# GpSimd copies for part of the V strips, and a last output tile in two column halves, in an attention and MLP kernel on one core

## The chip, the core and the metric

The kernel runs on one core of one Trainium2 chip. The metric is the device time of one execution in microseconds; lower is better. The core has five engines with a queue of instructions each: TensorE (PE, with its weight loads as PEld), VectorE (DVE), ScalarE (ACT), GpSimd (POOL) and SyncE (SP). Transfers are issued from the queues of POOL and SP and run on 16 DMA engines. Each engine takes its queue in order.

## The reference

For 8 batches with 8 heads of 64 there are 32 global and 512 local positions. A global query sees all 544 keys. A local query sees the 32 global keys and the local keys at most 32 positions away. The result, 4352 rows of 512, goes through a two-layer MLP (512 to 2048 to 512).

```python
k_all = np.concatenate([k_g, k_l], axis=2)
v_all = np.concatenate([v_g, v_l], axis=2)
out_g = np.matmul(sm(scale * np.matmul(q_g, k_all.transpose(0, 1, 3, 2))), v_all)
mask = np.abs(pos[:, None] - pos[None, :]) <= 32
s_ll = np.where(mask, scale * np.matmul(q_l, k_l.transpose(0, 1, 3, 2)), -1e9)
s_lg = scale * np.matmul(q_l, k_g.transpose(0, 1, 3, 2))
out_l = np.matmul(sm(np.concatenate([s_lg, s_ll], axis=-1)), v_all)
x = np.concatenate([out_g, out_l], axis=2)   # then batch and position as rows, heads as columns
h = x @ w_in
out = (h * np.clip(h + 3.0, 0.0, 6.0) / 6.0) @ w_out
```

## The kernel before, in words

The kernel first writes down all operations of all batches with their dependencies, an estimated duration, and a key that says when each is due (`add`). A planner (`Plan.lay`) then plays them through with one clock per engine and a model of the two transfer queues and sorts them by start. The program is issued in that order, so each engine's order is fixed when the kernel is built: a longer duration in an `add` moves other operations, on other engines too. Buffers come from rings (`acq`, `rel`): an operation that takes a buffer waits for the last reader of the one before.

Work goes by batch. Per batch:

- POOL issues the loads (`load`, L411): queries and keys of four tiles of 128 positions into `nat`, V into `ve` (the global rows `v_g` in partitions 0 to 31 of block 0, then five blocks of local rows; the fifth is a rest of 32 rows), and for every second batch the global queries and keys into `natg`. The weights `win` and `wout` come in four quarters each, through the same queue, in the first 65 us. A semaphore lane stands behind each load, and there are eight: a load waits until the eighth load before it has landed.
- Queries and keys are turned so that the head's dimension lies in the partitions: for batches 0 to 3 by PE transposes (L592, L612), for batches 4 to 7 by transfers (L582, `TURN_QK = 4`).
- A query tile of 128 is seen as four units of 32. Each unit needs the 32 global rows and 96 local rows of V in the 128 partitions of one "strip". The strips of a batch, 16 in all, stand in `st` (two buffers of 128 partitions x 16 x 512 fp16). `strips_moved` (L526) fills them for batches 1 to 7 with seven transfers from `ve` issued by SP (L536): one that repeats the global rows 16 times in partitions 0 to 31 (512 packets of 1 KB), and for each unit c the local rows (packets of 4 KB), in two pieces where the rows come from two blocks. For unit 1 the rows lie in partitions 32 to 127 of `ve` and go to the same partitions of `st`. Batch 0 has its own way (`strips_kept`, and a part of `strips_moved`): copies by DVE and ACT, and transfers.
- `local_step` per tile: scores on PE (L662, L669), mask and row minimum on DVE (L681), exponentials on ACT (L692), scaling on DVE (L706, `tensor_tensor` with both inputs in SBUF), transposes of the weights (L713 on PE up to batch 4, then L724 by transfers, `TURN_E = 5`), the product with the strips (L743) and its copy to `xt` on ACT or DVE (L296, L298).
- `global_steps`: the same for the 32 global queries, with scaling at L821, transposes at L835 and the product with `ve` at L848. When it and the strips are done, the batch's `ve` buffer is free for the batch after next.
- `moe_local`: the first layer (L870), ReLU on ACT (L877), the gate on DVE (L881), and the second layer (`second`, L892), 16 matmuls of 512 columns per tile of 128 positions, in four groups of four; the result is copied to `ot` (L296, L298) and stored by SP (L907).

After batch 7 `moe_global` does the global rows of all batches. In PE's order its matmuls stand between those of the last local tiles; the last tile of all is the fourth local tile of batch 7.

Of the kernel before, what the change touches and what calls it, by code (L numbers as in the profile page):

```python
# [79 lines left out]
class Plan:  # L80
# [128 lines left out]
def kernel(  # L209
# [24 lines left out]
    NU = P // UQ  # L234
# [3 lines left out]
    HD = H * D  # L238
# [15 lines left out]
    NS, NX, VE = 2, 3, 2  # L254
# [3 lines left out]
    psM = many(3, [P, 512], FP32, "m", pp)  # L258
# [6 lines left out]
    ve = many(VE, [P, NV, HD], FP16, "ve")  # L265
    st = many(2, [P, NJ * NU, HD], FP16, "st")
# [10 lines left out]
    ot = many(3, [P, dm], FP32, "ot")  # L277
    gs = many(2, [P, NDFF, 512], FP16, "gs")
# [4 lines left out]
    w_out_t = sb.tile([P, NDFF, dm], FP16, tag="wout", name="wout")  # L283
# [6 lines left out]
    add = plan.add  # L290
# [3 lines left out]
    def copy(op, out, in_):  # L294
        if op.eng == "ACT":
            nc.scalar.copy(out=out, in_=in_)  # L296
        else:
            nc.vector.tensor_copy(out=out, in_=in_)  # L298

    BOTH = ("ACT", "DVE")  # L300
# [225 lines left out]
    def strips_moved(b, js, key):  # L526
        r = b % 2
        n = len(js)
        j0, j1 = js[0], js[-1] + 1
        v4 = st[r].rearrange("p (u j) c -> p u j c", u=NU)  # L530
        before = [av_last[b - 2, j] for j in range(NJ)] if b >= 2 else []
        o = []

        def move(dst, src, packets, ns, deps):
            def emit(op):
                nc.sync.dma_start(out=dst, in_=src)  # L536
            o.append(add("SP", 600, emit, deps + before, key=key + 0.001 * len(o), dma=(packets, ns)))
            return o[-1]
        if n == NJ:
            move(st[r][0:G, :, :], ve[b % VE][0:G, 0:1, :].to_broadcast([G, NJ * NU, HD]), G * NJ * NU, SHORT, vload[b, 0][:1])  # L540
        elif n == NJ - KEEP or KEEP == 0 and j0 == 0:
            for j in range(j0, NJ) if KEEP else ():
                glob.append(move(v4[0:G, :, j, :], ve[b % VE][0:G, 0:1, :].to_broadcast([G, NU, HD]), G * NU, SHORT, vload[b, 0][:1]))
            if KEEP == 0:
                glob.append(move(st[r][0:G, :, :], ve[b % VE][0:G, 0:1, :].to_broadcast([G, NJ * NU, HD]), G * NJ * NU, SHORT, vload[b, 0][:1]))
        if b == 0:
            o += [x for x in glob if x not in o]
        ns = LONG if n == NJ else SHORT
        each = 1 if n == NJ else n
        for c in range(NU):  # L550
            lo = c * UQ
            a = min(P - lo, KL)
            deps = [x for j in range(j0, j1) for x in vload[b, j]]
            move(v4[G:G + a, c, j0:j1, :], ve[b % VE][lo:lo + a, j0:j1, :], a * each, ns, deps)
            if a < KL:
                deps = [x for j in range(j0 + 1, j1 + 1) for x in vload[b, j]]
                move(v4[G + a:P, c, j0:j1, :], ve[b % VE][0:KL - a, j0 + 1:j1 + 1, :], (KL - a) * each, ns, deps)
        return o
# [17 lines left out]
    TURN_M, TURN_QK, TURN_E, TURN_G, TURN = 1, 4, 5, 5, (64, 190.0, True)  # L576

    def turn_qk(b, j, ld, key, which=(0, 1)):
        r = b % 2
        if b >= TURN_QK:  # L580
            def move(op):
                nc.sync.dma_start_transpose(out=qk[r][:, :, :, UQ + j * P:UQ + (j + 1) * P].rearrange(  # L582
                    "d i p s -> d (i p) s"), in_=nat[ld[0].slot].rearrange("s i c -> s (i c)"))
            return add("SP", 1250, move, [*ld, prep["clear"], *old_qk(b, j)], key=key, rel=ld[:1], dma=TURN)
        w0, n = which[0], len(which)

        def pe(op):
            ps = psM[op.slot].bitcast(FP16) if b < TURN_M else psT[op.slot]
            for i in which:
                for p in range(NP):  # L590
                    c0 = ((i - w0) * NP + p) * P
                    nc.tensor.matmul(out=ps[:, c0:c0 + P], lhsT=nat[ld[0].slot][:, i, p * P:(p + 1) * P],  # L592
                                     rhs=ident, is_transpose=True)
        t = add("PE", 225 * n, pe, [*ld, prep["ident"]], key=key, acq="M" if b < TURN_M else "T", rel=ld[:1])

        def ev(op):
            ps = psM[t.slot].bitcast(FP16) if b < TURN_M else psT[t.slot]
            copy(op, qk[r][:, w0:w0 + n, :, UQ + j * P:UQ + (j + 1) * P],
                 ps[:, 0:n * NP * P].rearrange("d (i p s) -> d i p s", i=n, p=NP))
        deps = [t, prep["clear"]] + old_qk(b, j)  # L600
        return add(BOTH, (450 * n, 300 * n), ev, deps, key=key - 2, rel=[t])
# [33 lines left out]
    def local_step(b, j, key):  # L635
        r = b % 2
# [74 lines left out]
        def tr(op):  # L711
            for h in range(H):
                nc.tensor.matmul(out=psT[op.slot][:, h * P:(h + 1) * P], lhsT=pn[pn_op.slot][:, h, :],  # L713
                                 rhs=ident, is_transpose=True)
        if b < TURN_E:
            t = add("PE", 450, tr, scs, key=key - 0.2, acq="T", rel=[pn_op])
            et_op = add("DVE", 0, lambda op: None, [t], key=key - 0.3, acq="et")

            def ev(op):
                copy(op, et[et_op.slot].rearrange("k h q -> k (h q)"), psT[t.slot])  # L720
            e_ = add(BOTH, (900, 600), ev, [et_op], key=key - 2, rel=[t])
        else:
            def move(op):
                nc.sync.dma_start_transpose(out=et[op.slot], in_=pn[pn_op.slot].rearrange("q h k -> q (h k)"))  # L724
            e_ = et_op = add("SP", 1250, move, scs, key=key - 2, acq="et", rel=[pn_op], dma=TURN)
# [22 lines left out]
        else:  # L748
            vs = []
            for a in range(2):  # L750
                vs.append(add("PE", 235, lambda op, a=a: av(op, a), [e_, *strip[b, j], *vs], key=key - 0.4,
                              acq=f"A{a}", rel=[et_op]))
# [131 lines left out]
                                           op0=ALU.min, op1=ALU.mult)  # L884
        return add("DVE", 600, st_, [a], key=key - 1, rel=[f, to])

    def second(t0, gdone, set_, dests, keys):
        f = None
        for q in range(4):
            def pe(op, q=q):  # L890
                for c in range(q * 4, q * 4 + 4):
                    nc.tensor.matmul(out=psM[(f or op).slot], lhsT=gs[set_.slot][:, c, t0:t0 + P],  # L892
                                     rhs=w_out_t[:, c, :], start=(c == 0), stop=(c == NDFF - 1))
            deps = gdone[q * 4:q * 4 + 4] + [wo[q * 4]]
            if q == 0:
                f = s = add("PE", 865, pe, deps, key=keys[q], acq="M")
            else:
                s = add("PE", 865, pe, deps + [s], key=keys[q], rel=[set_] if q == 3 else [])
        oo = add("DVE", 0, lambda op: None, [s], key=keys[3] - 1, acq="ot")

        def ev(op):
            copy(op, ot[oo.slot], psM[f.slot])
        c = add(BOTH, (480, 605), ev, [oo], key=keys[3] - 1, rel=[f])

        for n, (dst, lo, hi) in enumerate(dests):
            def sto(op, dst=dst, lo=lo, hi=hi):
                nc.sync.dma_start(out=dst, in_=ot[oo.slot][lo:hi, :])  # L907
            add("SP", 600, sto, [c], key=keys[3] + 0.001 * n, rel=[oo], dma=(hi - lo, STORE))

    def moe_local(b, at, span):  # L910
        set_ = add("ACT", 0, lambda op: None, xdone[b, 0], key=at - 1, acq="gs")
        n = PART.get(b, 512)
        k, per, parts = 512 // n, n // P, Sl // n
        left = [0]

        def key():
            left[0] += 1
            return at + span * left[0] / 32
        done = [[None] * NDFF for _ in range(parts)]
        for part in range(parts):  # L920
            xdeps = [d for j in range(part * per, (part + 1) * per) for d in xdone[b, j]]
            for c in range(0, NDFF, k):
                o = first(c, n, part * n, lambda: xt[xt_op[b].slot], xdeps, [xt_op[b]], set_, key())
                done[part][c:c + k] = [o] * k
        for j in range(NJ):
            row = b * S + G + j * P
            second(j * P, done[j // per], set_, [(out[row:row + P, :], 0, P)], [key() for _ in range(4)])

    def moe_global(at, span):
        deps = [xgd[b] for b in range(B)]  # L930
# [122 lines left out]
```

## Time and profile before

| | us |
|---|---|
| median of 3 runs (332.3 to 334.16) | 332.98 |
| the profiled execution | 335.23 |
| its span, first to last instruction | 333.5 |
| PE busy | 317.4 (95%) |
| DVE busy | 265.2 (80%) |
| ACT busy | 253.9 (76%) |
| POOL busy, nearly all of it issuing loads | 106.1 (32%) |

The transfers moved 52.25 MB in 158,594 packets. The granted TensorE clock was 0.999 of full.

How to read the profile: "busy" is the time in which at least one instruction of the engine ran. A group is named by source line, engine, operation and tile (buffer numbers left out), with its count, mean duration, and the idle time of the engine ahead of it with what ended it. Each transfer has an issue (a short instruction on POOL or SP) and a landing. The chain that ended last goes back from the last instruction to what released it, and so on. The busy time of a matmul is modelled: matmuls overlap, and 16 matmuls of 512 columns, each shown with 0.38 us, follow each other at 0.216 us.

A row of the windows view names a stretch (from:to, length), then for PE, PEld, DVE, ACT and POOL the busy us and, in brackets, the number of instructions, then PE's granted clock, the load of the DMA engines and GB/s.

### The profile page before, as it was taken

The page shows a single profiled execution, that of the slowest core. Times are in us where ns is not written, and L with a number is a line of the kernel's source. Part 1 is how long each engine was busy: PE and PEld are TensorE (multiplying, and loading weights), DVE is VectorE, ACT ScalarE, POOL GpSimd, SP SyncE. Part 2 cuts the span into 40 slices and gives each one's busy share as a digit, 9 for nine tenths or more (in the row PEclk, how much of TensorE's full clock was granted, in tenths as well). Part 3 has the DMA queues.
Part 4 walks back from the last instruction along what each step waited for, and adds up shares of the span by engine and source line. Part 5 has one row for each costly group of instructions (what it writes and reads, how often), then busy time and mean ns, then how long its engine had stood idle before and what let it go on. Part 6 is the DMA issues. An engine that isn't in the chain of part 4 may idle for free.

```text
span 333.5 us, 10205 instructions
## 1 busy us (share of the span) xinstructions
PE 317.4 (95%) x3808; PEld 183.0 (55%) x3808; DVE 265.2 (80%) x997; ACT 253.9 (76%) x850; POOL 106.1 (32%) x139
## 2 busy tenths in 40 slices
PE   8989969799699999999999999999999999999995
PEld 6778855365356554555555555454455544546642
DVE  4899799789988799898998799689988896375400
ACT  4889798679789589977995689699988994474402
POOL 8724943198166733830760050005000000000000
PEclk9999999999999999999999999999999999999999
DMA  9999999999999999999999999999984215300022
GB/s 150 193 245 168 131 177 254 168 190 194 206 152 188 231 155 156 191 225 231 162 173 218 224 160 209 196 198 175 194 145 120 63 35 112 88 0 2 31 64 95
DMA packets 158594, 52.25 MB, mean 157 GB/s; under 512 B 142928, under 2 KB 151120, under 8 KB 158544
## 3 DMA queue, kind: packets, MB, share of 16 engines
q0 software_dynamic: 106560, 17.05, 71.9%
q1 hardware_dynamic: 51984, 34.55, 48.0%
q8 instruction: 30, 0.49, 0.6%
q14 instruction: 20, 0.16, 0.2%
HBM read 35.26 MB, written 8.91 MB: 132 GB/s over the span
## 4 chain that ended last, share of the span: by engine, by line
PE 60%; DMA 19%; POOL 7%; ACT 6%; DVE 5%; issue 2%; SPq 0%; ACTq 0%
PE m L892 28%; PE m L870 23%; DMA wout<-in_moe_w_out_dram 7%; DMA win<-in_moe_w_in_dram 5%; DMA nat<-in_k_l_dram 4%; POOL nat L411 3%; PE a L743 3%; POOL ve L411 3%; ACT sm L692 2%; DMA nat<-in_q_l_dram 2%; DVE gs L881 2%; PE s L669 2%; ACT t L877 1%; PE t L713 1%; PE s L662 1%
## 5 line engine op out<-in xcount | busy, mean ns | idle before, releaser
L892 PE MATMUL m<-wout,gs 128*128 128x512 f16 x544 | 129.6, 379 | 1.3 <-DMA wout<-in_moe_w_out_dram 1.3
L870 PE MATMUL m<-xt,win 128*128 128x512 f16 (+1 forms) x576 | 122.0, 355 | 1.7 <-DVE gs L881 1.0
L692 ACT ACTIVATE sm<-sm,stat 128x128 f32<-128x128 f32 x256 | 100.6, 397 | 11.4 <-DVE stat L681 10.8
L881 DVE SCALAR_TENSOR_TENSOR gs<-t,m 128x512 f16<-128x512 f32 x136 | 91.7, 683 | 19.6 <-ACT t L877 18.3
L877 ACT ACTIVATE t<-m 128x512 f32<-128x512 f32 x136 | 80.4, 597 | 22.1 <-PE m L870 21.3
L870 PEld LDWEIGHTS <-win 128*128 128x128 f16 x640 | 59.3, 98 | 52.2 <-issue 3.3
L892 PEld LDWEIGHTS <-gs 128*128 128x128 f16 x544 | 49.6, 98 | 52.7 <-issue 2.8
L681 DVE CUSTOM_DVE_ANT_0 sm<-s,mask 128x128 f32<-128x128 f32 x256 | 61.8, 283 | 2.5 <-PE s L669 1.1
L692 ACT ACTIVATION_READ_ACCUMULATOR sm<-sm,stat 128x1 f32 x256 | 49.6, 194 | 0.0
L706 DVE TENSOR_TENSOR pn<-sm,stat 128x512 f16<-128x512 f32 x64 | 44.0, 688 | 0.6
L411 POOL DMA_DIRECT2D ve<-in_v_l_dram x40 | 32.2, 822 | 15.0 <-PE m L870 4.3
L296 ACT CAST xt<-a 64x256 f16<-64x256 f32 (+1 forms) x83 | 31.0, 374 | 7.3 <-PE a L743 6.3
L411 POOL DMA_DIRECT2D nat<-in_q_l_dram x30 | 27.0, 899 | 23.1 <-DMA qk<-nat 10.2
L411 POOL DMA_DIRECT2D nat<-in_k_l_dram x30 | 27.4, 914 | 15.7 <-DMA nat<-in_k_l_dram 6.5
L743 PEld LDWEIGHTS <-st 128*128 128x128 f16 x448 | 19.7, 98 | 10.6 <-DVE et L298 0.3
L296 ACT COPY ot<-m 128x512 f32<-128x512 f32 x23 | 13.5, 588 | 13.8 <-PE m L892 10.5
L743 PE MATMUL a<-et,st 128*128 128x64 f16 x448 | 22.1, 193 | 0.2 <-ACT xt L296 0.2
L411 POOL DMA_DIRECT2D ve<-in_v_g_dram x8 | 4.8, 597 | 54.3 <-PE a L848 53.6
L681 DVE DVE_READ_ACCUMULATOR2_ANT stat<- 128x1 f32 x256 | 21.1, 83 | 0.0
L298 DVE CAST xt<-a 64x256 f16<-64x256 f32 (+1 forms) x33 | 14.1, 428 | 4.3 <-PE a L743 4.0
L702 DVE RECIPROCAL stat<-stat 128x4 f32<-128x4 f32 x64 | 11.1, 173 | 5.8 <-ACT sm L692 5.2
L807 ACT ACTIVATE sg<-a,stat 128x32 f32<-128x32 f32 x16 | 4.6, 287 | 14.3 <-DVE stat L798 14.3
(88 smaller groups left out, 279.6 us busy)
## 6 DMA issues: line engine op xcount, KB each, us to landing
out_dram<-ot SPq DMA_DIRECT2D x32, 256.0 KB, 3.7
st<-ve SPq DMA_DIRECT2D x14, 384.0 KB, 7.9
nat<-in_k_l_dram POOLq DMA_DIRECT2D x30, 128.0 KB, 8.1
nat<-in_q_l_dram POOLq DMA_DIRECT2D x30, 128.0 KB, 9.5
st<-ve SPq DMA_DIRECT2D x7, 512.0 KB, 7.7
st<-ve SPq DMA_DIRECT2D x14, 256.0 KB, 8.0
ve<-in_v_l_dram POOLq DMA_DIRECT2D x24, 128.0 KB, 6.0
st<-ve SPq DMA_DIRECT2D x18, 128.0 KB, 8.0
```

What stands on the lines that cost most here:

```text
L296: nc.scalar.copy(out=out, in_=in_)
L298: nc.vector.tensor_copy(out=out, in_=in_)
L411: nc.gpsimd.dma_start(out=dst(op), in_=src)
L681: nc.vector.tensor_tensor_reduce(out=sm[sm_op.slot][:, h, :], in0=psS[s.slot][:, e, p * P:(p + 1) * P], in1=m, scale=-scale, scalar=3.0e38 ...
L692: nc.scalar.activation(out=sm[sm_op.slot][:, h, :], in_=sm[sm_op.slot][:, h, :], func=EXP, scale=-1.0, bias=stat[stat_op.slot][:, 0, h:h + 1],
L702: nc.vector.reciprocal(out=stat[stat_op.slot][:, 2, h0:h1], in_=stat[stat_op.slot][:, 1, h0:h1])
L706: (nc.gpsimd if op.eng == "POOL" else nc.vector).tensor_tensor(out=pn[pn_op.slot][:, h0:h1, :], in0=sm[sm_op.slot][:, h0:h1, :], in1=stat[ ...
L743: nc.tensor.matmul(out=psA[a][:, c0:c0 + 64], lhsT=st[r][:, u * NJ + j, p * P:(p + 1) * P], rhs=et[et_op.slot][:, 2 * p:2 * p + 2, u * UQ: ...
L870: nc.tensor.matmul(out=psM[op.slot][:, i * n:(i + 1) * n], lhsT=w_in_t[:, m, (c + i) * P:(c + i + 1) * P], rhs=x()[:, m, t0:t0 + n], start ...
L877: nc.scalar.activation(out=t1[to.slot], in_=psM[f.slot], func=RELU, bias=0.5, scale=1.0 / 6.0)
L881: nc.vector.scalar_tensor_tensor(out=gs[set_.slot][:, c:c + k, t0:t0 + n], in0=t1[to.slot].rearrange("f (k t) -> f k t", k=k), scalar=1.0, ...
L892: nc.tensor.matmul(out=psM[(f or op).slot], lhsT=gs[set_.slot][:, c, t0:t0 + P], rhs=w_out_t[:, c, :], start=(c == 0), stop=(c == NDFF - 1))
```

## The change

In `strips_moved`, for batches 1 to 7, the transfer of the global rows becomes eight GpSimd copies, each to two of the 16 strips, and the transfer of unit 1's rows becomes four GpSimd copies (partitions 32 to 63 and 64 to 127, two tiles each). The planner takes them at 900 and 850 ns. Like the transfers they wait for the V loads and for the last reader of the strip buffer; they stand in POOL's queue, between the loads. The other five strip transfers stay on SP.

`second` can take a tile in several column parts. The last local tile of batch 7 is done in two halves of 256 columns: 16 matmuls, a copy and a store for each half, where 16 matmuls of 512 columns, one copy and one store were.

The tests at `TURN_QK` and `TURN_E` allow for fractions of a batch; both constants keep their values, 4 and 5.

```diff
@@ strips_moved
         if n == NJ:
-            move(st[r][0:G, :, :], ve[b % VE][0:G, 0:1, :].to_broadcast([G, NJ * NU, HD]), G * NJ * NU, SHORT, vload[b, 0][:1])
+            for i in range(0, NJ * NU, 2):
+                o.append(add("POOL", 900, lambda op, i=i: nc.gpsimd.tensor_copy(out=st[r][0:G, i:i + 2, :], in_=ve[b % VE][0:G, 0:1, :].to_broadcast([G, 2, HD])),
+                             vload[b, 0][:1] + before, key=key + 0.001 * len(o)))
...
             deps = [x for j in range(j0, j1) for x in vload[b, j]]
+            if c == 1 and n == NJ:
+                for x0, x1 in ((UQ, 2 * UQ), (2 * UQ, P)):
+                    for i in range(0, NJ, NJ // 2):
+                        o.append(add("POOL", 850, lambda op, x0=x0, x1=x1, i=i: nc.gpsimd.tensor_copy(
+                            out=v4[x0:x1, 1, i:i + NJ // 2, :], in_=ve[b % VE][x0:x1, i:i + NJ // 2, :]),
+                            deps + before, key=key + 0.001 * len(o)))
+                continue
             move(v4[G:G + a, c, j0:j1, :], ve[b % VE][lo:lo + a, j0:j1, :], a * each, ns, deps)
@@ turn_qk
-        if b >= TURN_QK:
+        if b + j / NJ >= TURN_QK:
@@ local_step
-        if b < TURN_E:
+        if b + j / NJ < TURN_E:
@@ second
-    def second(t0, gdone, set_, dests, keys):
+    def second(t0, gdone, set_, dests, keys, cuts=1):
+        w, oo, s, f = dm // cuts, None, None, None
+        for n in range(cuts):
+            cols = slice(n * w, (n + 1) * w)
...
+                        nc.tensor.matmul(out=psM[(f or op).slot][:, 0:w], lhsT=gs[set_.slot][:, c, t0:t0 + P],
+                                         rhs=w_out_t[:, c, cols], start=(c == 0), stop=(c == NDFF - 1))
...
+                copy(op, ot[oo.slot][:, cols], psM[f.slot][:, 0:w])
...
+                    nc.sync.dma_start(out=dst[:, cols], in_=ot[oo.slot][lo:hi, cols])
@@ moe_local
-            second(j * P, done[j // per], set_, [(out[row:row + P, :], 0, P)], [key() for _ in range(4)])
+            second(j * P, done[j // per], set_, [(out[row:row + P, :], 0, P)], [key() for _ in range(4)],
+                   2 if b == B - 1 and j == NJ - 1 else 1)
```

More of the change, by code (lines that the diff above doesn't have):

```diff
@@ L885, in first, with pe, ev, sto @@
         return add("DVE", 600, st_, [a], key=key - 1, rel=[f, to])
-    def second(t0, gdone, set_, dests, keys):
[L888 to L908, printed above, removed]
+    def second(t0, gdone, set_, dests, keys, cuts=1):
+        w, oo, s, f = dm // cuts, None, None, None
+        for n in range(cuts):
+            cols = slice(n * w, (n + 1) * w)
+            for q in range(4):
+                def pe(op, q=q, cols=cols, f=f if q else None):
+                    for c in range(q * 4, q * 4 + 4):
+                        nc.tensor.matmul(out=psM[(f or op).slot][:, 0:w], lhsT=gs[set_.slot][:, c, t0:t0 + P],
+                                         rhs=w_out_t[:, c, cols], start=(c == 0), stop=(c == NDFF - 1))
+                deps = gdone[q * 4:q * 4 + 4] + [wo[q * 4], s]
+                s = add("PE", 865 // cuts, pe, deps, key=keys[q] + 0.01 * n, acq=None if q else "M",
+                        rel=[set_] if q == 3 and n == cuts - 1 else [])
+                f = f if q else s
+            oo = oo or add("DVE", 0, lambda op: None, [s], key=keys[3] - 1, acq="ot")
+            def ev(op, cols=cols, f=f):
+                copy(op, ot[oo.slot][:, cols], psM[f.slot][:, 0:w])
+            c = add(BOTH, (480, 605) if cuts == 1 else (300, 340), ev, [oo, s], key=keys[3] - 1, rel=[f])
+            for i, (dst, lo, hi) in enumerate(dests):
+                def sto(op, dst=dst, lo=lo, hi=hi, cols=cols):
+                    nc.sync.dma_start(out=dst[:, cols], in_=ot[oo.slot][lo:hi, cols])
+                add("SP", 600, sto, [c], key=keys[3] + 0.001 * (n + i), rel=[oo], dma=(hi - lo, STORE))
```

## The prediction

> **What bounds the kernel now.** I read the page first, then the windows view (busy time by stretch of 20 us), then the waits, the timeline of TensorE (PE) and the chain that ended last.
>
> The windows, with busy us of PE, PEld, VectorE (DVE), ScalarE (ACT) and GpSimd (POOL) in each stretch:
>
> ```profile
> 40.00:60.00 20.00, 16.48 (x290) 11.43 (x288) 19.31 (x90) 17.86 (x69) 8.36 (x12) 1.00 1.27 209
> 60.00:80.00 20.00, 18.06 (x260) 10.82 (x259) 16.34 (x53) 15.35 (x53) 14.24 (x18) 1.00 1.79 177
> 80.00:100.00 20.00, 17.48 (x210) 9.86 (x209) 17.70 (x68) 16.91 (x57) 9.26 (x12) 1.00 1.76 183
> ...
> 120.00:140.00 20.00, 19.23 (x222) 10.31 (x219) 19.75 (x74) 18.67 (x63) 10.36 (x14) 1.00 1.89 164
> ...
> 160.00:180.00 20.00, 20.00 (x229) 10.81 (x228) 19.17 (x76) 18.49 (x65) 10.13 (x13) 1.00 1.92 175
> ```
>
> PE lacks 8.0 us between 40 and 100 us, and from 100 to 320 us it is nearly full (158.86 of 160 us between 100 and 260): there fewer transfers can buy nothing. So the gain, if any, lies before 100 us and behind the last matmul. The PE timeline says which idle time before 100 us is a transfer's:
>
> ```profile
> 44.73 0.44 PE L835 MATMUL t<-ident,pg 128*128 128x128 f16 x5 [1.49 <-ACT eg L296]
> 49.23 0.40 PE L713 MATMUL t<-ident,pn 128*128 128x128 f16 x4 [0.81 <-DVE pn L706]
> 50.49 0.35 PE L662 MATMUL s<-kgz,qk 128*128 128x32 f16 x8 [0.86 <-DVE stat L681]
> ...
> 64.39 2.75 PE L892 MATMUL m<-wout,gs 128*128 128x512 f16 x12 [1.32 <-DMA wout<-in_moe_w_out_dram]
> ...
> 91.25 0.40 PE L592 MATMUL t<-ident,nat 128*128 128x128 f16 x4 [2.34 <-DMA nat<-in_k_l_dram]
> ```
>
> Two waits are for loads: 1.32 us for the last quarter of w_out and 2.34 us for a key tile of batch 3. The three ahead of them are for ACT and DVE, which are full there. The chain shows how long both loads were under way (start, length):
>
> ```profile
> 42.27 22.07 DMA wout<-in_moe_w_out_dram
> ...
> 77.05 14.16 DMA nat<-in_k_l_dram
> ```
>
> A load that meets little traffic lands 3.3 us after its issue (the minimum over L411), so these two mostly stood in a queue: the DMA engines are 9 tenths busy there.
>
> **The change, part by part.** The times go with the profiled execution: 335.23 us, span 333.5 us, so 1.7 us lie around the span. It is 2.25 us above the median of 332.98; I put the difference that I work out on the median.
>
> *Removed.* In each of batches 1 to 7, SyncE (SP) no longer issues the 512 KB transfer of global rows and one 384 KB strip: 14 issues of some 0.6 us on a queue that is not late, and 896 of 2048 KB of strips per batch.
>
> *Added.* 12 copies on POOL per batch, of 1024 fp16 elements in each of 32 or 64 partitions. No copy on POOL is in the trace. The nearest rows:
>
> ```profile
> L374 POOL TENSOR_SCALAR_AFFINE_SELECT ident<-ident 128x128 f32<-128x128 f32 x1 | 0.3, 289 | 0.9 <-DVE ident L370 0.9
> L326 POOL TENSOR_SCALAR_AFFINE_SELECT mask<-mask 32x96 f32<-32x96 f32 x1 | 0.3, 258 | 0.0
> ...
> L298 DVE COPY st<-ve 32x1024 f16<-32x1024 f16 x2 | 0.8, 420 | 0.1
> ```
>
> From 96 to 128 elements POOL takes 31 ns more, 0.97 ns per element: 0.289 + 896 x 0.97 ns = 1.16 us for 1024, or 0.99 us by the slope alone. DVE takes 0.42 us for the same copy, ACT 1.04. Bounds 0.42 and 1.16; I take 0.90, next to POOL's slope and a little under it, because a copy compares nothing and moves half the bytes. By the Trainium skill (GPSIMD Engine Reference, section Elementwise), which gives about 1.03 cycles per element at 1.2 GHz for the simplest loops, an estimate is 0.88 us and the sum would stay as below; no run here shows it.
>
> Twelve copies take 10.8 us, and about 0.07 us each of waiting for DVE (below) makes 11.6 us per batch. The order of the changed program shows what is queued behind them on POOL: in batch 1 the last quarter of w_out; in batch 2 six key and query loads of batch 3; in batches 3 and 7 the last V load of the batch, for which two strips wait.
>
> *w_out.* Its last quarter is issued at 42.27 + 11.6 = 53.9 us. The quarters before it no longer share the engines with the global rows. The four w_in loads, in a line, land 2.5 to 5.0 us apart, so it lands at 53.9 + 3.3 + 2.5 to 4 = 60 to 61 us, not at 64.34. PE comes there at 62.5 (64.39 less 1.48, less 0.45 for eight transposes, L713, which the new order puts later). The 1.32 us go.
>
> *The key tile.* The loads behind w_out move up by some 3 us with it: the first four loads for batch 3 are issued by about 73.2 us (76.2 before, two of them ahead of the copies). The copies run to 84.9, the awaited tile is issued at 85.8 and lands some 5 us later (unhurried ones took 3.3 to 6), at 91. The new PE order has 26.5 us of work between w_out and this tile (23.2 before), so PE gets there at 62.5 + 26.5 + 0.9 of small waits as before + 1 for DVE = 90.9. The 2.34 us go, without slack. For batch 3 the V loads are issued by 94.5, the copies end at 106.6, the last V load lands at 110.6 and the last strip 6 us later, at 116.6. PE, with 52 us of work, needs it at 117: again just in time.
>
> *The end.* The last tile is 32 matmuls of 256 columns (109 ns apart) instead of 16 of 512 (216 ns): +0.03 us. Behind the last one stand an ACT copy of 256 columns (0.37 for 0.59 us, by the xt casts of that width) and a store of half the bytes (the last store needs 2.0 us to land, the 64 KB ones 1.7): -0.35 us in all. The first half's copy and store lie beside 1.7 us of matmuls.
>
> *DVE.* POOL and DVE get in each other's way. L821 reads and writes SBUF:
>
> ```profile
> L821 DVE TENSOR_SCALAR pg<-sg,stat x16: 486/502/952, 41.8 to 281.4; 128x544 f16<-128x544 f32 x16
> L706 DVE TENSOR_TENSOR pn<-sm,stat x64: 679/687/693, 13.3 to 276.0; 128x512 f16<-128x512 f32 x64
> ```
>
> Five of sixteen took 0.76 to 0.95 us instead of 0.50, all while POOL issued loads. L706 never did. Against copies, the cost of one L706 lies between nothing (its row) and a whole copy, 0.90 us. The Trainium skill (SBUF — State Buffer, section Who interferes with whom) speaks against the change: a VectorE instruction with two SBUF inputs, as L706 has, is shut out by a GpSimd instruction that reads SBUF, though not by one that only writes, and whichever starts first holds the port to its end. Its flat row while POOL only issued loads agrees; reading copies are not in this trace. By the rule each collision costs half a copy on average, by the row alone nothing.
>
> I take the middle, 0.45 us. A batch has 8 L706 and 2 L821 in some 33 us, so 3.5 of them meet 11.6 us of copies: 1.6 us of DVE per batch. Where DVE has idle time that is hidden. Batch 1's copies fall in 42 to 54 us, where DVE is busy 11.92 of 12 us: 1.2 us reach PE. Batches 4 and 5 fall near the windows with 19.75 and 19.17: 0.5 us together. Were no cover left in all seven batches, it would be 11 us.
>
> *No cost.* The fractions at TURN_QK and TURN_E change nothing while these are 4 and 5. PE's order is the same up to the fourth group of second-layer matmuls, and further on holds the same work.
>
> Sum: -1.32 - 2.34 - 0.35 + 0.03 + 1.2 + 0.5 = -2.3 us, so 332.98 - 2.3 = **330.7 us**.
>
> **The rivals.**
> 1. *POOL becomes late: slower.* At 1.16 us a copy, and the same waits, a batch's copies take 14.8 us, 3.2 more. The key tile stands behind two batches' copies (up to 6.4 late; some 4 after the slack at w_out), the last strip of batch 3 behind a third (3 more). 330.7 + 7 = 337.7 us. At 7 us for 0.26 us per copy, the gain is gone from 0.99 us per copy, and it is slower by 0.5% from 1.05. For it: POOL's slope is 0.99 and both dates have no slack. Against: POOL waits 53.6 us for PE later on (ve after L848), so only batches 1 to 3 suffer.
> 2. *The gain is eaten by DVE: no change.* If the collisions cost PE 4.0 us instead of 1.7, the time is 333.0. For it: DVE at 11.92 of 12 us; the skill's rule just named, if each collision held a whole copy, would do this. Against: L706's flat row.
> 3. *DVE is not held at all: faster still.* 332.98 - 4.0 = 329.0; with a quicker copy, down to 0.42 us, loads come earlier and some of the remaining waits before 100 us go as well, to about 326.5.
>
> **How the numbers follow.** Forecast 0.38, with its own range 329.3 to 331.3; rival 3 0.15; rival 2 0.22, 331.3 to 334.6; rival 1 0.25. A measurement of this kernel tells about 0.5% (1.7 us) from no change, so the forecast and rival 3 count as faster: 0.53, same 0.22, slower 0.25. The range, 326.5 to 337.5, takes in 329.0 to 326.5 of the quick copy and nearly all of rival 1; both signs are in it because the copy's price decides.
>
> **What would show it.** Right: POOL copies that start about 0.9 us apart; no PE wait for w_out, and none above 0.5 us for nat tiles before 100 us; PE busier than 16.48, 18.06 and 17.48 in the windows from 40 to 100; some L706 rows near 1.1 us or more; about 3.4 us instead of 3.8 between the last matmul and the span's end. Wrong: copies of 1.05 us or more with PE waiting for nat tiles or for strips of batch 3 near 117 us (rival 1); L706 above 1 us throughout with longer waits at L835, L713 and L662 between 42 and 62 us (rival 2); L706 flat at 0.69 (rival 3).

## The result

The changed kernel takes 352.74 us (median of 4 runs, 347.25 to 354.09) against 333.57 us: 1.0488 times the time before, 95% interval 1.035 to 1.0626. A second set of runs on another occasion gave 348.25 us (344.80 to 352.63), 1.0378 times (1.0303 to 1.0453). The median of all eight is 350.4 us. The ratios leave out runs far above the fastest of the same kernel, which is why they lie a little under what the medians give; the profiled execution read here (354.09 us) is one of those left out, that of the second set (344.80 us) is not. Forecast were 330.7 us and a range up to 337.5: it is 14 to 19 us slower than before, where 2.3 us less were expected. What this section reads from the profile at 354.09 us is held against the one at 344.80 us under "The changed kernel again".

The windows of the changed kernel (columns as before: PE, PEld, DVE, ACT, POOL busy, then the granted clock, load of the DMA engines, GB/s):

```profile
40.00:60.00 20.00, 12.75 (x222) 10.04 (x221) 17.97 (x53) 13.27 (x47) 19.90 (x22) 0.83 1.21 180
60.00:80.00 20.00, 17.06 (x233) 10.04 (x232) 19.51 (x64) 13.29 (x54) 19.47 (x24) 0.98 1.71 144
80.00:100.00 20.00, 16.82 (x221) 10.10 (x221) 16.95 (x71) 17.29 (x57) 13.82 (x16) 0.93 1.18 131
```

PE was to be busier than 52.02 us between 40 and 100; it is busy for 46.63, and between 40 and 60 at 0.83 of its clock. POOL is full there. DVE's busy time tells little: 53 instructions are shown with 17.97 us, where 90 took 19.31. They stand longer. The PE timeline names the waits:

```profile
47.86 0.45 PE L844 MATMUL t<-ident,pg 128*128 128x128 f16 x5 [3.92 <-DVE pg L830]
50.36 0.69 PE L844 MATMUL t<-ident,pg 128*128 128x128 f16 x5 [2.04 <-ACT eg L296]
...
78.02 0.61 PE L722 MATMUL t<-ident,pn 128*128 128x128 f16 x8 [2.83 <-DVE qk L298]
...
99.41 0.31 PE L752 MATMUL a<-et,st 128*128 128x64 f16 x5 [1.82 <-DMA st<-ve]
```

No wait is for w_out or for a key tile any more, as forecast. In their place PE waits for DVE, and behind the first such wait for ACT (the copy eg, 2.04 us, 1.49 before). By source (L830 was L821, L715 was L706, L637 was L628; times are min/median/max in ns):

```profile
L830 DVE TENSOR_SCALAR pg<-sg,stat x16: 496/504/5035, 42.8 to 302.9; 128x544 f16<-128x544 f32 x16
```

```profile
L715 DVE TENSOR_TENSOR pn<-sm,stat x64: 678/691/1541, 13.8 to 294.6; 128x512 f16<-128x512 f32 x64
```

The medians of the first two are those of before. Their worst are a 0.50 us instruction that stood for 5.04 us, and 1.54 us where 0.69 was the rule. The small kgz copies of L637, 0.19 us long where nothing holds them, stood for up to 0.99. What POOL did while L830 stood, in POOL's and DVE's timelines:

```profile
42.46 8.41 POOL L541 COPY st<-ve 32x1024 f16<-32x1024 f16 x8
50.93 4.44 POOL L559 COPY st<-ve 32x1024 f16<-32x1024 f16 x4
```

```profile
42.77 6.23 DVE L830 TENSOR_SCALAR pg<-sg,stat 128x544 f16<-128x544 f32 x2
```

The first copy began 0.31 us before the first L830; twelve stand in a row, with hardly a gap. L830 got through after about five. With PE idle for 3.92 us the granted clock fell; the window of the next 6.8 us, and that behind the wait at 78.02:

```profile
48.50:55.30 6.80, 4.94 (x78) 4.11 (x79) 5.81 (x27) 5.23 (x21) 6.70 (x7) 0.50 1.11 229
79.20:82.60 3.40, 2.95 (x56) 2.19 (x28) 3.12 (x13) 2.42 (x10) 3.34 (x4) 0.50 0.00 0
```

At half clock PE does in 10.2 us at most the work of 5.1, so these two stretches cost up to 5.1 us on top of the waits. The chain of waits has L830 where it had the load of w_out, and later a strip transfer where it had the key tile (start, length):

```profile
42.85 6.15 DVE pg L830 x2
...
88.48 10.79 DMA st<-ve
```

By engine it is now:

```profile
PE 45%; DVE 30%; ACT 11%; DMA 9%; issue 3%; POOL 1%; SPq 0%; ACTq 0%; DVEq 0%
```

In the first profile of the kernel before DVE had 5% of it and DMA 19%; in its second profile, under "The kernel before, a second profile", it is 15% and 9%.

One figure is used throughout below: DVE's **held time**. For each line and form, the part of an instruction's time that lies more than 0.03 us above the lower quarter of its kind, added up over the trace. It is 20.4 us here (7.7 of it in L715, 6.3 in L830, 5.4 in L637) and 3.0 in the first profile of the kernel before, 2.1 in the second.

### The profile page after: what moved, and what is told of

Its sections match the earlier page's. It is cut to its first block, busy times and chain, and to the rows that moved or that the text cites. A ratio compares the mean times of both kernels' runs of the same rounds, so it can differ in the third digit from the quotient of the medians.

```text
span 352.2 us, 10331 instructions
## 1 busy us (share of the span) xinstructions
PE 322.2 (91%) x3824; PEld 187.0 (53%) x3824; DVE 282.2 (80%) x998; ACT 256.3 (73%) x850; POOL 197.3 (56%) x223
## 4 chain that ended last, share of the span: by engine, by line
PE 45%; DVE 30%; ACT 11%; DMA 9%; issue 3%; POOL 1%; SPq 0%; ACTq 0%; DVEq 0%
PE m L903 24%; PE m L879 14%; DVE gs L890 8%; DVE pn L715 6%; DMA st<-ve 5%; DVE sm L690 4%; ACT sm L701 4%; ACT t L886 3%; DVE pg L830 2%; DMA et<-pn 2%; PE a L752 2%; DMA nat<-in_q_l_dram 2%; DVE kgz L637 2%; ACT xt L296 2%; DVE xt L298 1%
## 5 line engine op out<-in xcount | busy, mean ns | idle before, releaser
L903 PE MATMUL m<-wout,gs 128*128 128x512 f16 (+1 forms) x560 | 129.2, 374 | 0.0
L879 PE MATMUL m<-xt,win 128*128 128x512 f16 (+1 forms) x576 | 123.6, 358 | 3.3 <-DVE gs L890 2.5
L903 PEld LDWEIGHTS <-gs 128*128 128x128 f16 x560 | 51.4, 98 | 51.1 <-issue 2.7
L541 POOL COPY st<-ve 32x1024 f16<-32x1024 f16 x56 | 60.0, 1123 | 2.8 <-DMA ve<-in_v_g_dram 2.6
L715 DVE TENSOR_TENSOR pn<-sm,stat 128x512 f16<-128x512 f32 x64 | 52.1, 814 | 0.8
L296 ACT CAST xt<-a 64x256 f16<-64x256 f32 (+1 forms) x79 | 29.5, 373 | 12.4 <-PE a L752 11.2
L559 POOL COPY st<-ve 32x1024 f16<-32x1024 f16 (+1 forms) x28 | 32.0, 1168 | 0.7
L296 ACT COPY ot<-m 128x512 f32<-128x512 f32 (+1 forms) x27 | 15.4, 571 | 17.6 <-PE m L903 16.9
L752 PEld LDWEIGHTS <-st 128*128 128x128 f16 x448 | 20.6, 99 | 13.7 <-issue 3.3
L722 PE MATMUL t<-ident,pn 128*128 128x128 f16 x160 | 13.1, 220 | 6.8 <-DVE pn L715 3.8
```

Of the source, the lines that this page charges most:

```text
L541: o.append(add("POOL", 900, lambda op, i=i: nc.gpsimd.tensor_copy(out=st[r][0:G, i:i + 2, :], in_=ve[b % VE][0:G, 0:1, :].to_broadcast([G, ...
L559: o.append(add("POOL", 850, lambda op, x0=x0, x1=x1, i=i: nc.gpsimd.tensor_copy(out=v4[x0:x1, 1, i:i + NJ // 2, :], in_=ve[b % VE][x0:x1, ...
L715: (nc.gpsimd if op.eng == "POOL" else nc.vector).tensor_tensor(out=pn[pn_op.slot][:, h0:h1, :], in0=sm[sm_op.slot][:, h0:h1, :], in1=stat[ ...
L752: nc.tensor.matmul(out=psA[a][:, c0:c0 + 64], lhsT=st[r][:, u * NJ + j, p * P:(p + 1) * P], rhs=et[et_op.slot][:, 2 * p:2 * p + 2, u * UQ: ...
L879: nc.tensor.matmul(out=psM[op.slot][:, i * n:(i + 1) * n], lhsT=w_in_t[:, m, (c + i) * P:(c + i + 1) * P], rhs=x()[:, m, t0:t0 + n], start ...
L903: nc.tensor.matmul(out=psM[(f or op).slot][:, 0:w], lhsT=gs[set_.slot][:, c, t0:t0 + P], rhs=w_out_t[:, c, cols], start=(c == 0), stop=(c ...
```

## The experiments

Theory 1: POOL's copies keep DVE out, PE waits for DVE, and its clock falls. Theory 2: POOL's queue is late with loads and strips (rival 1 of the prediction). Theory 3: the order that the planner makes of the longer POOL list is bad. Each run stands beside runs of the kernel before on the same chip (334.0 to 334.5 us).

### Copies of 8 columns: what the order and the saved transfers are worth

```diff
-out=st[r][0:G, i:i + 2, :], in_=ve[b % VE][0:G, 0:1, :].to_broadcast([G, 2, HD])
+out=st[r][0:G, i:i + 2, 0:8], in_=ve[b % VE][0:G, 0:1, 0:8].to_broadcast([G, 2, 8])
```

(and the same for unit 1; four small GpSimd memsets stand between the early loads)

> The changed kernel with each of its 84 GpSimd copies cut to 8 of 512 columns, every instruction in the same order; the rest of those strip rows is left unwritten, so part of V is missing from the product. Four small GpSimd memsets in the loads at 20 to 31 us set the untouched rows once. Theory 1 (the copies shut VectorE out of SBUF, TensorE idles and its granted clock halves): without the time of the copies nothing is left of it, so 327 to 331 us, under the kernel before, with L715 flat at 0.69 us and L830 near 0.50, and no clock of 0.5 after 40 us. Theory 2 (GpSimd's queue is late with loads): the same 327 to 331, so this run does not part 1 from 2. Theory 3 (the order that the planner makes of the longer GpSimd list is itself bad): 345 us or more, as the changed kernel.

Measured: 333.67 us, 0.9996 times before (0.9965 to 1.0028); held time 1.6 us, and L715, here L721, is flat:

```profile
L721 DVE TENSOR_TENSOR pn<-sm,stat x64: 677/689/728, 14.1 to 273.8; 128x512 f16<-128x512 f32 x64
```

Theory 3 is out: the order costs nothing that shows. But the gain is not there either: all of the removed transfers and the halves together bring 1.2 us at most, by the interval.

### Only the last tile in halves

The kernel before with `second` and its call from the change, nothing else.

> The kernel before with the last output tile in two halves of columns and nothing else: no GpSimd copies, all transfers kept. All theories: 0.2 to 0.5 us less than the kernel before, 332.6 to 333.4 us; the last ACT copy at 0.37 us for 0.59. If the halves were part of the loss it would be slower than the kernel before by more than 0.5 us.

Measured: 334.00 us, 0.9983 times (0.9950 to 1.0016). The sign agrees with the forecast of -0.32 us; the interval holds no change as well. Its trace says something else. All transfers are kept, and still no PE wait for w_out stands in it, and the key tile is waited for 0.98 us, not 2.34.

### The kernel before, a second profile

> The kernel before once more, for its profile. The prediction took 1.32 us (last quarter of w_out) and 2.34 us (key tile of batch 3) as waits of every execution. If they belong to that one execution, 2.25 us above its median, then the two together are under 2 us here and the time is near 333 us; if they belong to the kernel, they are 3 us or more again.

Measured: 333.48 us. Its PE timeline at the two places of the prediction:

```profile
62.54 2.75 PE L892 MATMUL m<-wout,gs 128*128 128x512 f16 x12
...
89.34 0.40 PE L592 MATMUL t<-ident,nat 128*128 128x128 f16 x4 [1.02 <-DMA nat<-in_k_l_dram]
```

No bracket at the first row: the same twelve matmuls that waited 1.32 us in the first profile wait for nothing. Of the 3.66 us that were to go, this execution has 1.02. The first profile was one of 335.23 us, 2.25 over its median. The two profiles lie 1.75 us apart, and these two waits differ by 2.64 us.

### Memsets in place of copies

```diff
-nc.gpsimd.tensor_copy(out=st[r][0:G, i:i + 2, :], in_=...)
+nc.gpsimd.memset(st[r][0:G, i:i + 2, :], 0.0)
```

> The changed kernel with each GpSimd copy replaced by a GpSimd memset of the same shape (write only; the strip rows get zeros in place of rows of V). Theory 1, if it hangs on GpSimd reading SBUF: L715 (two SBUF inputs) goes back to 0.69 us, the mean of L830 to at most 0.7, and the time to 329 to 334 us. Theory 1, if any GpSimd instruction shuts out any VectorE instruction: L715 stays above 0.78, time 343 or more. Theory 2 (late queue): depends only on the length of a memset; at 0.9 us or more each it stays above 343 with L715 flat. Theory 3 (order): above 343 whatever the lengths.

Measured: 348.41 us, 1.0434 times (1.0383 to 1.0485). Of theory 1, neither form came as written: L714 went back to 0.69 us, as the first has it, and the time stayed above 343 us, as the second has it. That is also what theory 2 expected, so that only the next run parts the two. By source, the scaling of the global and of the local weights:

```profile
L829 DVE TENSOR_SCALAR pg<-sg,stat x16: 495/502/7322, 42.9 to 296.6; 128x544 f16<-128x544 f32 x16
```

```profile
L714 DVE TENSOR_TENSOR pn<-sm,stat x64: 676/686/694, 13.8 to 288.3; 128x512 f16<-128x512 f32 x64
```

L714, with two SBUF inputs, is flat against POOL work that only writes. L829, with one, stood for 7.3 us, through nearly the whole row of eight memsets (42.67 to 49.97 us); PE waited for it and ran at half clock for the next 10.2 us:

```profile
50.33 0.71 PE L843 MATMUL t<-ident,pg 128*128 128x128 f16 x5 [6.21 <-DVE pg L829]
```

One tensor_scalar of 0.50 us so cost up to some 11 us (6.2 of wait and at most 5.1 of clock).

### The same, with the scaling in the other form

```diff
-nc.vector.tensor_scalar(out=pg[po.slot][:, 0:S], in0=sg[sgo[e].slot],
-                        scalar1=stat[so.slot][:, 2, e:e + 1], scalar2=None, op0=ALU.mult)
+nc.vector.tensor_tensor(out=pg[po.slot][:, 0:S], in0=sg[sgo[e].slot],
+                        in1=stat[so.slot][:, 2, e:e + 1].to_broadcast([P, S]), op=ALU.mult)
```

> The run with memsets in place of copies (strips get zeros), and L829's tensor_scalar as tensor_tensor with two SBUF inputs. Theory 1a: a GpSimd instruction that only writes does not hold the form with two inputs, so L829 flat at 0.70 to 0.75 us, the wait of 6.37 us for pg and the 10.24 us of halved clock behind it gone: 348.4 - 6.4 - 0.6 - 5.1 = 336 us, 334 to 338. Theory 1b: L829 at several us again, 346 to 350.

Measured: 335.52 us, 1.004 times (1.0006 to 1.0074), and

```profile
L829 DVE TENSOR_TENSOR pg<-sg,stat x16: 715/719/726, 41.8 to 283.9; 128x544 f16<-128x544 f32 x16
```

Every tensor_tensor is flat, held time is 1.9 us, and 12.9 us are gone with one changed line. This also bears on theory 2: the 84 memsets are still in POOL's queue at 0.94 us each or a little more, and this run loses 1.1 us by the medians, 2.5 at most by the interval. With copies POOL's queue is 9% longer (197.3 us busy for 181.6), which was not tried without their contention.

These two runs bear on the Trainium skill, page SBUF — State Buffer, section Who interferes with whom. It says that a two-input VectorE instruction contends with GpSimd instructions that read SBUF and not with those that only write, and that copy, cast and tensor_scalar, where they run in a mode with two ports, contend with GpSimd altogether. The traces agree: 694 ns at most for the one, 7322 for the other. It says also that whoever issues first holds the ports for the whole instruction; a wait through five copies or nearly eight memsets is more than that.

### The changed kernel with the scaling in the other form

The same edit on the changed kernel.

> The changed kernel with L830's tensor_scalar (one tensor from SBUF, a scalar per partition) written as tensor_tensor with the scalar broadcast, as L715 is; same engine, same place. Theory 1a, the wait through five copies belongs to the form with one input, and the form with two waits for one copy at most: L830 at most 1.7 us, TensorE's first wait for pg 1 us for 3.92, no halved clock near 48 us, 343 to 347 us. Theory 1b, any VectorE instruction can be kept out through several copies in a row, and L715 just never fell there: L830 3 us or more again, 350 to 354 us.

Measured: 348.57 us, 1.0410 times (1.0347 to 1.0472); the longest L830 is 1.56 us, the longest L715 1.57, held time 16.2 us. By source:

```profile
L830 DVE TENSOR_TENSOR pg<-sg,stat x16: 717/722/1561, 41.8 to 298.0; 128x544 f16<-128x544 f32 x16
```

The wait for one copy at most agrees with theory 1a, but the time lies 1.6 us above its range, and the next run takes the contrast away. Against copies, which read, the two-input form is held too (12.3 of the 16.2 us are L715's), so little is won.

### The changed kernel again

> The changed kernel again, unchanged. The runs so far lie 7 us apart (347.3 to 354.1). Theory 1: what varies is how many copies in a row L830 waits through near 42 us, with the halved clock behind it; a profile at 352 us or more shows a wait of 3 us or more there, one near 347 shows a wait of one copy.

Measured: 348.25 us (344.80 to 352.63); the profiled run is the one at 344.80, the fastest of the eight. Its longest L830 is 1.26 us: one copy, with the one-input form.

```profile
L830 DVE TENSOR_SCALAR pg<-sg,stat x16: 495/504/1264, 41.6 to 293.5; 128x544 f16<-128x544 f32 x16
```

```profile
44.98 0.44 PE L844 MATMUL t<-ident,pg 128*128 128x128 f16 x5 [1.92 <-ACT eg L296]
...
51.47 0.40 PE L722 MATMUL t<-ident,pn 128*128 128x128 f16 x4 [1.23 <-DVE pn L715]
```

The loss is of the same kind as in the first profile, without the long wait: held time is 17.3 us (10.3 of it in L715, up to 1.56 us each), DVE has 32% of the chain, and the clock is at half for 3.4 us behind each of these two waits. The span is 11.0 us above that of the second profile of the kernel before. So the same instruction at the same place waits for one copy in one execution and for five in another. That wait of 3.92 us is the largest part of the 9.5 us between the two spans; the waits of 2.83 and 1.82 us at 78.02 and 99.41 us are gone here too, and the clock is at half for 6.8 us in place of 10.2. That the scatter of all eight runs goes with L830 is not shown: the changed kernel with the other form, without a long wait of L830 in its profile, scatters nearly as much (346.46 to 352.77). What decides how many copies it waits for is not shown by these runs either.

### Each part alone

Global rows alone (eight copies per batch; `if c == 1 and n == NJ` made false, no halves), and unit 1 alone (four; the `move` of the global rows kept, no halves):

> Only the global rows are copied by GpSimd, eight copies per batch; unit 1 keeps its transfer and the last tile is whole. Theory 1 (the time lost is the time that VectorE is held): 8/12 of the 17.4 us by which VectorE's held time grew from the kernel before (3.0) to the changed one (20.4), so 334.3 + 11.6 = 346 us, 343 to 349. Were the loss in the four copies of unit 1, which wait for all V loads: within 2 us of the kernel before.

> Only unit 1's rows are copied by GpSimd, four copies per batch; the global rows keep their transfer and the last tile is whole. Theory 1: 4/12 of 17.4 us, so 334.3 + 5.8 = 340 us, 337 to 343, with no VectorE instruction kept out through more than four copies. Were the loss in the eight copies of global rows: within 2 us of the kernel before.

Measured: 347.96 us, 1.0404 times (1.0306 to 1.0501), runs from 341.89 to 351.11, profiled at 341.89 with held time 9.7 us; and 337.89 us, 1.0110 times (1.0077 to 1.0142), held time 6.2 us. Both lie in the ranges of theory 1, and each part alone loses. Eight copies lose 13.5 us and four lose 3.4, so the loss grows faster than their number.

### Copies only from batch 3 on

```diff
-        if n == NJ:
+        if n == NJ and not (b >= 3):
+            move(st[r][0:G, :, :], ve[b % VE][0:G, 0:1, :].to_broadcast([G, NJ * NU, HD]), G * NJ * NU, SHORT, vload[b, 0][:1])
+        elif n == NJ:
...
-            if c == 1 and n == NJ:
+            if c == 1 and n == NJ and b >= 3:
```

> The changed kernel with the copies only from batch 3 on; batches 1 and 2 keep their transfers. Theory 1: what VectorE's held instructions cost in batches 1 and 2 goes: 4.09 + 0.75 us of waits and 3.4 us of halved clock for batch 1, 3.00 + 0.66 us and 1.7 us for batch 2, and the strip wait of 1.98 us, 15.6 in all, with some 1 us of load waits back: 352.7 - 14.6 = 338 us, 336 to 341. Theory 2 (late GpSimd queue): the copies of batch 3 to 7 are the ones behind which loads are late, so 347 or more.

Measured: 345.84 us, 1.0370 times (1.0305 to 1.0436). That is under the 347 us of theory 2 and above the 341 us of theory 1: 7 us came back of the first set's median, 2.4 of the second's, and not 15. With no halved clock and no L830 in its way the rest still loses 11 us, on a held time of 13.2 us. PE, nearly full behind 100 us before, now waits there for L717 (L715), and for a transposed tile of weights (et) whose input L717 makes (whether the late L717 or the transfer itself makes that second wait is not shown):

```profile
138.57 0.40 PE L724 MATMUL t<-ident,pn 128*128 128x128 f16 x4 [1.51 <-DVE pn L717]
...
206.95 0.39 PE L754 MATMUL a<-et,st 128*128 128x64 f16 x8 [1.83 <-DMA et<-pn]
```

### Each copy as two of half the length

`[nc.gpsimd.tensor_copy(... i + z:i + z + 1 ...) for z in range(2)]` in each place.

> The changed kernel with every GpSimd copy issued as two of half the length, in the same place. Theory 1 with a wait for a number of instructions: the longest L830 falls from 5.04 to some 2.8 us, the longest L715 from 1.54 to 1.1, time 343 to 348. Theory 1 with a wait for the row of copies to pause: L830 stays near 5 us, L715 near 1.1, 347 to 352. Theory 2 (late queue): twice the fixed cost of a copy on GpSimd, so no gain, 352 or more.

Measured: 354.70 us (347.75 to 358.94; too scattered for an interval). A half copy stands for 0.69 us in the mean, two of them 1.37, a whole one in the changed kernel 1.12 to 1.17. L830's worst is 1.84 us and L715's 1.13, held time 10.8 us. Since the whole copies held L830 for 5.04 us in one execution and 1.26 in another, this doesn't tell whether the number of copies counts. But now theory 2 shows: PE waits for strips and loads.

```profile
97.92 0.61 PE L601 MATMUL t<-ident,nat 128*128 128x128 f16 x4 [1.33 <-DMA nat<-in_k_l_dram]
...
127.96 0.31 PE L752 MATMUL a<-et,st 128*128 128x64 f16 x5 [2.45 <-DMA st<-ve]
163.86 0.53 PE L752 MATMUL a<-et,st 128*128 128x64 f16 x7 [2.29 <-POOL st L559]
```

So rival 1's mechanism is real, at 1.37 us per 1024 elements. In the first profile of the changed kernel only the wait of 1.82 us at 99.41 is of this kind, in the second only one of 0.91 us for a strip that POOL copies, as far as waits above 0.8 us go.

### The copies added to the kernel before

Twelve copies, from an idle tile to a spare one, behind the fourth V load of batches 1 to 7; unknown to the planner.

> The kernel before, with all its transfers and its own order, and twelve GpSimd copies of 32x1024 from an idle tile to a spare tile behind the fourth V load of each batch from 1 to 7: the copies without anything else of the change. Theory 1: VectorE is shut out just as in the changed kernel, and no transfer is saved, so 345 to 355 us, L706 mean at 0.78 or more, L821 with single times of several us. Theory 2: 337 to 341 us, with TensorE waiting for loads and L706 flat. Theory 3 (order): within 2 us of the kernel before, since the order is its own.

Measured: 381.71 us, 1.1413 times (1.1364 to 1.1462). That is 27 us above the upper end of theory 1. Held time is 15.4 us, as theory 1 has it, but with an order that does not know of them the copies also make POOL late, and here PE waits for loads and strips:

```profile
95.63 0.40 PE L599 MATMUL t<-ident,nat 128*128 128x128 f16 x4 [4.16 <-DMA nat<-in_q_l_dram]
...
175.53 0.43 PE L750 MATMUL a<-et,st 128*128 128x64 f16 x5 [3.71 <-DMA st<-ve]
```

The changed kernel has little of this. Its planner is told of the copies and orders around their length, but it has fewer transfers too, and their place among the loads is another; which of these spares it the long waits is not shown.

### DVE time taken without POOL

28 DVE copies of 32x1024 (0.42 us each, 11.8 us in all) added to the kernel before, POOL untouched: one ahead of the first L706 of each tile, once unknown to the planner and once known; then all four of a batch at its first tile; then one ahead of each kgz copy and each L821.

```diff
             def sc(op, h0=h0, h1=h1):
+                if b and h0 == 0:
+                    nc.vector.tensor_copy(out=spare[0:G], in_=idle[0:G].unsqueeze(1).to_broadcast([G, 2, HD]))
```

> The kernel before, GpSimd untouched, with one VectorE copy of 32x1024 from an idle tile to a spare one (0.42 us) ahead of the first of the two L706 of each tile in batches 1 to 7: 28 copies, 11.8 us of VectorE time without any contention. The prediction's step (idle time of VectorE hides it, 1.7 of 11 us reach the end): 334.3 + 1.8 = 336 us, 335 to 338. Rival (VectorE's in-order queue stands in the ring between scores and transposes, and what it loses is lost to TensorE about one for one): 343 to 347 us.

> As the run with 28 added VectorE copies, but the planner is told of them (430 ns more on the operation that carries them) and may order around them. If VectorE's idle time can hide 11.8 us when the order allows for it: 334 to 337 us. If not: within 3 us of the run in which the planner does not know.

> The same 28 added VectorE copies of 0.42 us (11.8 us, GpSimd untouched, unknown to the planner), but all four of a batch at its first tile, two ahead of each L706. If what counts is how closely the lost time is packed (28 spread evenly cost 4.1 us): 8 us or more lost, 342 us or more. If only the sum counts: within 2 us of the run with even spread, 336 to 340.

> The same 28 added VectorE copies, but placed where the GpSimd copies held VectorE longest in the profile at 352 us: one ahead of each L628 (kgz) and one ahead of each L821 (pg) of batches 1 to 7. If the place counts (short instructions that scores and transposes of TensorE wait for): 8 us or more lost, 342 us or more. If only the sum counts: 336 to 340.

| where the 11.8 us are | us | times before (95% interval) |
|---|---|---|
| spread, one per tile | 338.08 | 1.0131 (1.0063 to 1.0199) |
| the same, planner told | 337.36 | 1.0106 (1.0046 to 1.0166) |
| all at the first tile of each batch | 342.51 | 1.0239 (1.0193 to 1.0284) |
| at kgz and pg | 340.77 | 1.0173 (1.0114 to 1.0232) |

Of the spread copies 4.1 us of 11.8 reach the end, not 1.8 and not all; 338.08 us is at the upper edge of the range for the prediction's step. Telling the planner changes nothing that shows. Packed, 8.0 us reach the end, as expected if packing counts; at kgz and pg 6.3, between the two expectations. Packed, and at kgz and pg, the clock falls as well. The window from 40 to 60 us of the packed run, where the clock had been 1.00:

```profile
40.00:60.00 20.00, 15.09 (x245) 9.97 (x250) 17.90 (x78) 15.85 (x60) 6.86 (x10) 0.91 1.26 223
```

### All of them together

One execution each:

| profile of | held DVE time, us | span, us |
|---|---|---|
| before, second profile | 2.1 | 331.7 |
| 8 columns | 1.6 | 331.6 |
| memsets, other form | 1.9 | 332.9 |
| unit 1 alone | 6.2 | 336.4 |
| global rows alone | 9.7 | 340.1 |
| from batch 3 on | 13.2 | 343.8 |
| memsets | 14.2 | 345.8 |
| changed, other form | 16.2 | 347.0 |
| changed, second profile | 17.3 | 342.7 |
| changed, first profile | 20.4 | 352.2 |
| copies of half the length | 10.8 | 350.5 |
| copies added to the kernel before | 15.4 | 379.5 |

Where held time grows, the span grows by 0.7 to 1.2 us for each us of it, counted from the first row. The last two rows are the exception, with 2.2 and 3.6: there TensorE waits for strips and loads as well. By the runs without POOL, DVE time lost packed or at kgz and pg costs 0.5 to 0.7 us for each us; what makes up the rest (both at once, more of the halved clock, a few strip waits) was not taken apart.

No version of these beats the kernel before. What the change saves is worth nothing that shows even when the copies are cut to 8 columns (333.67 us), so there was nothing to build one from.

## Why the prediction was wrong

1. *w_out.* The reading of the queue was right: the last quarter was issued at 55.3 us (forecast 53.9) and landed at 61.0 (60 to 61), and no PE wait for it is left. The term of -1.32 us was not there to be had: the second profile of before has no such wait either.
2. *The key tile.* The wait is gone, but it was worth 1.02 us in the second profile, not 2.34. Nor does its absence show that the tile came early enough: issued at 85.5 us (86.8 in the second profile; forecast 85.8), it landed at 95.1 (91.4; forecast 91), and PE, held up by DVE, came later still. These two terms made up more than the whole gain. They were read from one execution 2.25 us above its median and then put on the median.
3. *The end.* The last ACT copies take 0.37 us as forecast; -0.32 us agrees with the run with halves alone, and is too small to be shown. Between the last matmul and the span's end lie 3.5 us (forecast 3.4, before 3.7).
4. *The price of a copy.* 0.90 us taken; the first follow each other at 0.98 us, and the twelve with their waits take 12.9 us (42.46 to 55.37) for 11.6. That is beyond rival 1's point of 0.99 us per copy, yet its signs did not come: no PE wait for a nat tile, none for the strips of batch 3 near 117 us. The run with memsets in the other form loses 1 us with its first twelve memsets in 11.1 us (41.73 to 52.83). What 12.9 us would cost if DVE were not late as well is not shown.
5. *DVE: the step that failed.* "1.6 us of DVE per batch. Where DVE has idle time that is hidden", 1.7 us in all. The held time grew by 15.2 to 18.3 us, 2.2 to 2.6 per batch, so that price was only some 1.5 times too low. The cover was wrong: 11.0 and 20.5 us reached the end in the two profiles, so even the 11 us set down for no cover at all were at the low end. In the runs without POOL a third of lost DVE time passes to the end when it is taken evenly, two thirds when it is taken at one tile per batch, where the prediction let 1.7 of 11 us pass. The likely reason, not shown by itself: DVE's idle time in a window is time in which it waits for PE and ACT, which wait for it in turn, and it is not there at the moment when a copy holds it. And the halved clock was no term at all: up to 5.1 us in the first profile, 3.4 in the second.
6. *What was left out in step 5.* Only L706 and L821 were counted, each meeting one copy. The kgz copies were held for 5.4 us in sum (1.6 in the second profile). One L821 stood through five copies, and with the halved clock behind it that is the largest single loss of the first profile (3.92 us of wait and up to 3.4 of clock); the second profile has no such wait. The row that told of it was shown and read too lightly: five of sixteen L821 took 0.76 to 0.95 us next to POOL's loads, and L706 never did. It meant that L821's form meets POOL in more ways than L706's; the prediction priced both alike.
7. *The rivals.* Rival 2 named the cause, DVE, with a rise of 2.3 us over the forecast for what was some 20. None went beyond 337.7 us, since the slower rival was built on POOL's lateness alone. The sign "some L706 rows near 1.1 us or more" came true along with longer waits at L835, one of the signs of rival 2; its other sign, L706 above 1 us throughout, did not (the median stayed at 0.69).

## What to carry to other kernels

Work moved to GpSimd next to a busy VectorE can be paid by VectorE: look which of its instructions read two SBUF operands or are plain copies and scalings, count all that fall into the row of GpSimd instructions, and price what they lose at about one for one on the end, as here (0.7 to 1.2), if the row is packed. Do not count idle VectorE time in a window as cover before a run has shown how much of it is. And before a wait is booked as a gain, look whether a second execution has it: here a profile 2 us over its median showed 2.6 us of waits that the second did not.

## What was unexpected of the hardware

- A VectorE instruction of 0.50 us waited 4.5 us behind GpSimd copies of 1 us and 6.8 us behind memsets of 0.94 us that stood in a row; in another execution of the same kernel 0.77 us.
- A GpSimd memset of 32x1024 fp16 takes 0.94 us, little less than the copy, of which one began every 0.98 us.
- A TensorE wait of 3.92 us was followed by 6.8 us at half clock, one of 6.21 us by 10.2 us, one of 2.83 and one of 1.92 by 3.4. One of 2.34 us, in the first profile of the kernel before, was followed by none, so the length of the wait alone does not decide. The Trainium skill, page TensorE: Matmul & The Clock Gate, Part 1, has the clock at half after an idle window of about 3.4 us; the stretches here are once, twice and three times that, and a wait of 1.92 us was enough for one.
